# Window attention, forward and backward, on one core: weights loaded in rows and turned on TensorE, both projections ahead of attention in the first steps, weight-gradient groups of one quad at the end

## The chip, the cores and the metric

One core of a Trainium2 chip. The metric is the device time of one execution in microseconds, the median of several. Kernels are compared only within the same rounds.

## The reference, cut to what matters

```
qkv = window(x) @ wqkv                # x: 256 x 256 x 384, windows of 8 x 8 pixels
p   = softmax(q k^T * 384**-0.5)      # 64 x 64 per window
out = (p v) @ wo                      # first result
dx, dwqkv, dwo = vjp(grad_out)        # the other three
```

The kernel never forms q, k and v. It forms four products of weights once: A = scale Wq Wk^T, its transpose AT, B = Wv Wo, its transpose BT. It works on "quads" of eight windows (512 rows), 128 of them, in a software pipeline.

## The kernel before: the parts that count

A quad n needs its x and grad_out in rows (X, DO), both turned (XT, DOT, by DMA transpose), both projected (A on XT, BT on DOT, evicted to YHT) and the projections turned back (YH, by DMA transpose). All DMA transposes are issued on SyncE's queue, in program order. The kernel puts TensorE's products into eight PSUM banks (PS). Where new products go into a bank that is still full, the trace shows TensorE waiting until ScalarE (ACT) or VectorE (DVE) has evicted the old ones, that is, copied them out (three waits for ACT at the end of before, 2.3 us together). TM and PB are tiles of the softmax chain, OS and DXS hold the evicted first result and dX.

```python
def load_x(q, n):        # four DMAs of 96 KB, issued on the queue of engine q
    for t in range(4):
        q.dma_start(out=X[:, (n % NX) * 4 + t, :], in_=img(x, n, t))
# load_do: the same for DO.  turn_in(n, 0 or 1): SP.dma_start_transpose of X to XT, of DO to DOT
# turn_yh(n, a): SP.dma_start_transpose of YHT to YH

def step(n):
    T, S, A = n, n + 1, n + 2            # attention, scores, projections of three quads
    ...                                  # doT, doS, doA; doF: there is a finished group of three quads
    load_do(SP, n + 4); load_x(POOL, n + 4)
    turn_in(n + 3, 0); turn_in(n + 3, 1)
    if doS: scores(S)
    if doT: md(T)
    if doS: chain0(S)                    # softmax, first part (DVE)
    if doF:
        wgrad(g, k0)                     # weight gradient: 12 matmuls
    elif doA:
        proj(A, 0, (7, 4, 5, 3), ...)    # projection of X: 12 matmuls
        turn_yh(A, 0)
    if doS:
        chain2(S); chain3(S)             # softmax and its gradient (ACT, DVE, POOL)
    if doT:
        outs(T, 0, 0, ACT)               # result 0 into banks 0, 1; evicted by ACT to OS
        outs(T, 2, 2, ACT)               # banks 2, 3
        outs_st(T)
    if doF:
        wgrad(g, k0 + 1)
        if doA: ...                      # proj(A, 0), turn_yh(A, 0) here in full steps
    if doT:
        attn_all(T, S if doS else None)  # needs chain3 of T+1's scores to be off its bank (TM), and P of S (PB)
        dxs(T, 0)
        dxs_ev(T, 0, ACT)                # dX, first half, evicted by ACT to DXS
    if doA or A == 0:
        stack(A, 0, 0, 3)
        proj(A, 1, (3, 4, 5, 7), ...)    # projection of DO
        ...
        turn_yh(A, 1)
    if doT:
        dxs(T, 1)                        # second half; shares a bank with the first
        dxs_ev(T, 1, ACT)

# the start
for m in range(CK):
    SP.dma_start_transpose(out=wT[:, 0:2 * CK, ...], in_=wqkv[m * P:(m + 1) * P, 0:2 * C])   # Wq, Wk
load_x(ACT, 0)
ACT.dma_start(out=wo_sb[:], ...)
load_do(POOL, 0)
turn_in(0, 0)
for m in range(CK):
    SP.dma_start_transpose(out=wT[:, 2 * CK:, ...], in_=wqkv[m * P:(m + 1) * P, 2 * C:])     # Wv
turn_in(0, 1)
load_x(SP, 1)
...                                      # 14 matmuls that nobody reads (4.70 us)
wprod(A_sb, ...)
gate(A_sb[0:1, 2, 0:1])                  # POOL waits for A, then:
load_do(POOL, 1)
turn_in(1, 0); turn_in(1, 1)
proj(0, 0, ...); turn_yh(0, 0)
wprod(BT_sb, ...)
gate(BT_sb[0:1, 2, 0:1])
step(-2)                                 # load_do(SP, 2), load_x(POOL, 2), proj(0, 1), turn_yh(0, 1)
scores(0); chain0(0); chain2(0); chain3(0)
wprod(AT_sb, ...); wprod(B_sb, ...)
for n in range(-1, NQ): step(n)
...                                      # (cut) weights reloaded in rows at n == 4 for the end

# the end: weight-gradient groups of three quads, the last of two, all of it after the last step
for n in range(NQ, GQ * NG + GQ):
    for i in range(2):
        wgrad(n // GQ - 1, 2 * (n % GQ) + i, ...)
```

Of the kernel before, what the change touches and what calls it, by code (L numbers as in the profile page):

```python
# [11 lines left out]
BF16 = mybir.dt.bfloat16  # L12
# [4 lines left out]
def kernel(  # L17
# [11 lines left out]
    nc = tc.nc  # L29
    _, H, W, C = x.shape  # L30
    P = 128
    CK = C // P
# [3 lines left out]
    NQ = (H // 16) * NQC  # L36
    scale = float(C) ** -0.5
    GQ = 3
    NG = (NQ + GQ - 1) // GQ
    NX, ND, NXT, NDT, NYH, NTOK, NVW = 11, 5, 3, 2, 2, 3, 6  # L40
    PE, DVE, ACT, POOL, SP = nc.tensor, nc.vector, nc.scalar, nc.gpsimd, nc.sync

# [61 lines left out]
    def turn_yh(n, a):  # L104
        SP.dma_start_transpose(out=YH[:, n % NTOK, a, :, :],
                               in_=YHT[:, n % NYH, a, :, :].rearrange("p m t -> p (m t)"))

    def proj(n, a, banks, engs):
        wgt = A_sb if a == 0 else BT_sb
        src = (XT[:, n % NXT] if a == 0 else DOT[:, n % NDT]).rearrange("p (t m) k -> p m t k", m=CK)  # L110
        i = 0
        for mo in range(CK):
            for t0, t1 in ((0, 4),) if mo < CK - 1 else ((0, 2), (2, 4)):
                o = PS[:, banks[i], 0:P * (t1 - t0)]
                for m in range(CK):
                    mm(o.rearrange("p (t k) -> p t k", k=P), wgt[:, m, mo * P:(mo + 1) * P], src[:, m, t0:t1, :],
                       m == 0, m == CK - 1)
                ev(engs[i], YHT[:, n % NYH, a, mo, P * t0:P * t1], o)
                i += 1
# [134 lines left out]
            for w in range(2):  # L254
                POOL.dma_start(out=img(out_1, n, t)[8 * w:8 * w + 8], in_=DXS[64 * (1 - w):64 * (1 - w) + 64, n % 2, t, :])  # L255

    def wgrad(g, k, bank=7):
        quads = range(g * GQ, min(NQ, (g + 1) * GQ))
        which, ma = k // CK, k % CK
        tiles = [(q, t) for q in quads for t in range(4)]  # L260
        for i, (q, t) in enumerate(tiles):
            mm(PS[:, bank, 0:C], X[:, (q % NX) * 4 + t, ma * P:(ma + 1) * P], VW[:, (q % NVW) * 4 + t, which, :],
               i == 0, i == len(tiles) - 1)
        if g == 0:
            DVE.tensor_copy(out=ACC[:, k, :], in_=PS[:, bank, 0:C])
        else:
            DVE.tensor_tensor(out=GF[:, k, :] if g == NG - 1 else ACC[:, k, :], in0=PS[:, bank, 0:C],
                              in1=ACC[:, k, :], op=ALU.add)

    flat = VW[:].rearrange("p a b c -> p (a b c)")  # L270
    wT = flat[:, 0:JK * C].rearrange("p (j c) -> p j c", j=JK)
# [3 lines left out]
    bank = [0]  # L275
# [12 lines left out]
    def step(n):  # L288
        T, S, A = n, n + 1, n + 2
        doT, doS, doA = 0 <= T < NQ, 0 < S < NQ, 0 < A < NQ  # L290
        g, k0 = n // GQ - 1, 2 * (n % GQ)
        doF = 0 <= g < NG
        if 1 < n + 4 < NQ:
            load_do(SP, n + 4)
            load_x(POOL, n + 4)
        if 1 < n + 3 < NQ:
            turn_in(n + 3, 0)
            turn_in(n + 3, 1)
        if doS:
            scores(S)  # L300
        if doT:
            md(T)
        if doS:
            chain0(S)
        if doF:
            wgrad(g, k0)
        elif doA:
            proj(A, 0, (7, 4, 5, 3), (ACT, ACT, ACT, DVE))
            turn_yh(A, 0)
        if doS:  # L310
            chain2(S)
            chain3(S)
        if doT:
            outs(T, 0, 0, ACT)
            outs(T, 2, 2, ACT)
            outs_st(T)
        if doF:
            wgrad(g, k0 + 1)
            if doA:
                proj(A, 0, (3, 1, 2, 5), (ACT, ACT, ACT, DVE))  # L320
                turn_yh(A, 0)
        if doT:
            attn_all(T, S if doS else None)
            dxs(T, 0)
            dxs_ev(T, 0, ACT)
        if doA or A == 0:
            stack(A, 0, 0, 3)
            proj(A, 1, (3, 4, 5, 7), (ACT, ACT, ACT, DVE))
            stack(A, 1, 0, 2)
            stack(A, 1, 2, 3)  # L330
            turn_yh(A, 1)
        if doT:
            dxs(T, 1)
            dxs_ev(T, 1, ACT)
        elif S == 0:
            turn_p(S)
            turn_p_ev(S)

    def gate(ap):
        POOL.tensor_copy(out=ST[0:1, 3, 0:1], in_=ap)  # L340

    with tc.manual_schedule():

        wsrc = TM[:].rearrange("p t k -> p (t k)").bitcast(BF16)
        DVE.memset(wsrc, 0.0)
        ACT.activation(out=SS[:], in_=TM[:], func=ACTF.Exp)
        for m in range(CK):
            SP.dma_start_transpose(out=wT[:, 0:2 * CK, m * P:(m + 1) * P], in_=wqkv[m * P:(m + 1) * P, 0:2 * C])
        load_x(ACT, 0)
        ACT.dma_start(out=wo_sb[:], in_=wo.rearrange("(m p) n -> p m n", p=P))  # L350
        make_identity(nc, ident[:])
        load_do(POOL, 0)
        turn_in(0, 0)
        for m in range(CK):
            SP.dma_start_transpose(out=wT[:, 2 * CK:, m * P:(m + 1) * P], in_=wqkv[m * P:(m + 1) * P, 2 * C:])  # L355
        turn_in(0, 1)
        load_x(SP, 1)
        for i in range(14):
            mm(PS[:, 7, :], wsrc[:, 0:P], wsrc, True, True)
        wprod(A_sb, wT[:, 0:CK], wT[:, CK:2 * CK], True)  # L360
        gate(A_sb[0:1, 2, 0:1])
        load_do(POOL, 1)
        turn_in(1, 0)
        turn_in(1, 1)
        proj(0, 0, (0, 1, 2, 3), (ACT, DVE, ACT, DVE))
        turn_yh(0, 0)
        wprod(BT_sb, wo_sb, wT[:, 2 * CK:3 * CK], False)
        gate(BT_sb[0:1, 2, 0:1])
        step(-2)
        scores(0)  # L370
        chain0(0)
        chain2(0)
        chain3(0)
        wprod(AT_sb, wT[:, CK:2 * CK], wT[:, 0:CK], True)
        wprod(B_sb, wT[:, 2 * CK:3 * CK], wo_sb, False)
        for n in range(-1, NQ):
            step(n)
            if n == 4:
                for m in range(CK):
                    SP.dma_start(out=w_sb[:, m, :], in_=wqkv[m * P:(m + 1) * P, :])  # L380
                    SP.dma_start_transpose(out=woT_sb[:, :, m * P:(m + 1) * P], in_=wo[m * P:(m + 1) * P, :])


        b = 0
        for n in range(NQ, GQ * NG + GQ):
            for i in range(2):
                wgrad(n // GQ - 1, 2 * (n % GQ) + i, (3, 4, 5, 6, 7)[b % 5])
                b += 1

        def ep(o, lt, rr, dst, eng, sc):  # L390
            for mb in range(CK):
                mm(o, lt(mb), rr(mb), mb == 0, mb == CK - 1)
            if eng is ACT:
                ACT.activation(out=dst, in_=o, func=ACTF.Copy, scale=scale if sc else 1.0)  # L394
            elif sc:
                DVE.tensor_scalar(out=dst, in0=o, scalar1=scale, scalar2=None, op0=ALU.mult)
            else:
                DVE.tensor_copy(out=dst, in_=o)

        def tr(h):  # L400
            for mb in range(CK):
                pt = PS[:, h * CK + mb, :].bitcast(BF16)
                for ma in range(CK):
                    PE.transpose(pt[:, ma * P:(ma + 1) * P], GF[:, h * CK + ma, mb * P:(mb + 1) * P], ident[:])
                ev(DVE if mb % 2 == 0 else ACT, GFT[:, h * CK + mb, :], pt[:, 0:C])

        dw = flat[:, 0:CK * J].rearrange("p (m j) -> p m j", m=CK)
        dwo = flat[:, CK * J:CK * J + CK * C].rearrange("p (m j) -> p m j", m=CK)
        cut = lambda ma: slice(ma * P, (ma + 1) * P)
        tr(0)  # L410
        for ma in range(CK):
            ep(PS[:, 6 + ma % 2, 0:C], lambda mb: GF[:, mb, cut(ma)], lambda mb: w_sb[:, mb, C:2 * C],
               dw[:, ma, 0:C], DVE if ma == 1 else ACT, True)
        tr(1)
        for ma in range(CK):
            ep(PS[:, ma, 0:C], lambda mb: GFT[:, mb, cut(ma)], lambda mb: w_sb[:, mb, 0:C],
               dw[:, ma, C:2 * C], DVE if ma == 0 else ACT, True)
        SP.dma_start(out=out_2.rearrange("(m p) j -> p m j", p=P)[:, :, 0:2 * C], in_=dw[:, :, 0:2 * C])
        for ma in range(CK):
            ep(PS[:, 6 + ma % 2, 0:C], lambda mb: w_sb[:, mb, 2 * C + ma * P:2 * C + (ma + 1) * P],  # L420
               lambda mb: GF[:, CK + mb, :], dwo[:, ma, :], DVE if ma == 1 else ACT, False)
        ACT.dma_start(out=out_3.rearrange("(m p) n -> p m n", p=P), in_=dwo[:])
        for ma in range(CK):
            ep(PS[:, 3 + ma, 0:C], lambda mb: GFT[:, CK + mb, cut(ma)], lambda mb: woT_sb[:, mb, :],
               dw[:, ma, 2 * C:3 * C], DVE if ma == 1 else ACT, False)
            SP.dma_start(out=out_2[cut(ma), 2 * C:3 * C], in_=dw[:, ma, 2 * C:3 * C])
# [30 lines left out]
```

## Time and profile before

| | before |
|---|---|
| time, median of 3 | 1999.05 us (1997.54 to 2000.05) |
| TensorE busy | 1968.3 of 1997.9 us |
| a full step | 15.16 us, no wait of TensorE |
| first scores product of step 3 (the first full step) | 83.91 us |
| last scores product to the end of the span | 48.72 us |

The page's first part, busy time of each engine with its share of the span and its number of instructions:

```profile
PE 1968.3 (99%) x27496; PEld 1311.8 (66%) x27496; DVE 1341.4 (67%) x2962; ACT 1301.0 (65%) x2321; POOL 1291.7 (65%) x2312
```

One stretch of 15 us in the middle, in the windows view (columns: stretch, its length, busy time and instructions of PE, weight loads, DVE, ACT and POOL, granted TensorE clock (1.00 is full), DMA share, GB/s):

```profile
1000.00:1015.00 15.00, 15.00 (x215) 10.06 (x213) 10.28 (x23) 9.94 (x19) 10.07 (x18) 1.00 1.08 214
```

In the middle TensorE is busy for all of the 15 us at full clock. A change that leaves a full step alone can gain at the two ends only.

The start, in the timeline (start us, duration, engine, line, operation, and in brackets the idle time before it and what ended it). "SPq" is SyncE's queue issuing a DMA; a transpose XT<-X is one quad's turn.

```profile
11.07 1.42 SPq L101 DMA_TRANSPOSE XT<-X  x1
12.54 4.20 SPq L355 DMA_TRANSPOSE VW<-in_wqkv_dram  x3
16.90 1.46 SPq L101 DMA_TRANSPOSE DOT<-DO  x1
18.41 2.88 SPq L93 DMA_DIRECT2D X<-in_x_dram  x4
23.72 1.62 SPq L101 DMA_TRANSPOSE XT<-X  x1
...
31.80 4.34 POOL L93 DMA_DIRECT2D X<-in_x_dram  x8
...
38.64 2.39 SPq L101 DMA_TRANSPOSE XT<-X  x1
...
43.81 4.00 PE L75 MATMUL PS<-XT,A_sb 128*128 128x512 bf16 x12 [4.00 <-DMA XT<-X]
```

Quad 0's X is turned at 11.07, quad 1's at 23.72, quad 2's at 38.64. TensorE then waits 4.00 us for the last of these; it can project quad 2 only when the turn has landed, at 43.8.

Who held TensorE up from 36 to 90 us (waits: total us, times, longest), which is steps 0 to 2 and the start of step 3:

```profile
PE PS L75 <- DMA XT<-X: 4.7, 2, 4.0
PE PS L75 <- DVE TM L157: 2.4, 3, 1.4
PE PS L169 <- POOL PB L160: 1.2, 3, 0.6
...
```

The end: the waits from 1949 to 1990 us.

```profile
PE PS L75 <- ACT DXS L79: 2.3, 3, 0.9
PE PS L75 <- DVE ACC L267: 0.7, 2, 0.4
...
```

And the block of weight-gradient matmuls that stands behind the last step, in the timeline:

```profile
1974.61 11.86 PE L75 MATMUL PS<-VW,X 128*128 128x384 bf16 x72
```

TensorE waits 3.0 us in the last steps, and 11.9 us of work that could have filled those waits comes after them.

### The profile page before, as it was taken

The numbers are of one execution on the slowest core, as the hardware profiler recorded it, in microseconds if no ns is written. First come the engines' busy times: TensorE is split into PE (matmuls) and PEld (weight loads), VectorE is DVE, ScalarE is ACT, GpSimd is POOL, SyncE is SP. The second block draws the span as 40 slices with busy tenths as digits, with TensorE's granted clock in tenths as the row PEclk, the third lists the DMA queues.
The fourth block names the chain that finished last, engine by engine and source line by source line (L and its number), as shares of the span: only waits on it lengthen the run. The fifth ranks groups of instructions, "written<-read, shape, count | busy, mean of one in ns | idle before, by whom it ended". The sixth has DMA issues, their size and how long they took to land.

```text
span 1997.9 us, 68536 instructions
## 1 busy us (share of the span) xinstructions
PE 1968.3 (99%) x27496; PEld 1311.8 (66%) x27496; DVE 1341.4 (67%) x2962; ACT 1301.0 (65%) x2321; POOL 1291.7 (65%) x2312
## 2 busy tenths in 40 slices
PE   6999999999999999999999999999999999999998
PEld 3666666666666666666666666666666666666665
DVE  3676667667666666766666676676666667666664
ACT  2766666666666666666666666666666666666664
POOL 2766666666666666666666666666666666666653
PEclk8999999999999999999999999999999999999999
DMA  9999999999999999999999999999999999999993
GB/s 175 217 222 219 221 211 216 211 207 211 205 206 215 214 199 221 210 212 204 213 205 216 208 212 209 209 210 208 210 212 205 218 204 213 209 211 209 209 170 73
DMA packets 982127, 411.06 MB, mean 206 GB/s; under 512 B 865200, under 2 KB 956848, under 8 KB 981808
## 3 DMA queue, kind: packets, MB, share of 16 engines
q1 hardware_dynamic: 882128, 254.31, 78.4%
q0 software_dynamic: 98304, 151.39, 29.1%
q8 instruction: 215, 3.52, 0.7%
q10 hardware_dynamic: 1376, 0.98, 0.2%
q14 instruction: 104, 0.85, 0.2%
HBM read 101.84 MB, written 101.84 MB: 102 GB/s over the span
## 4 chain that ended last, share of the span: by engine, by line
PE 96%; DMA 1%; DVE 1%; ACT 1%; POOL 0%; SPq 0%; issue 0%; ACTq 0%; POOLq 0%; DVEq 0%
PE PS L75 95%; PE PS L169 2%; DMA X<-in_x_dram 1%; DMA XT<-X 0%; DMA DOT<-DO 0%; SPq L355 0%; DVE TM L157 0%; POOL PB L160 0%; ACT VW L394 0%; ACT YHT L79 0%; POOL UM L159 0%; ACT DXS L79 0%; POOL X L93 0%; ACT MD L79 0%; DVE PB L155 0%
## 5 line engine op out<-in xcount | busy, mean ns | idle before, releaser
L255 POOL DMA_DIRECT2D out_dram<-DXS x1024 | 577.9, 570 | 408.1 <-ACT DXS L79 380.5
L75 PE MATMUL PS<-VW,X 128*128 128x384 bf16 x3072 | 541.6, 326 | 0.0
L79 ACT CAST YHT<-PS 128x512 bf16<-128x512 f32 x767 | 370.5, 517 | 244.3 <-PE PS L75 229.8
L75 PEld LDWEIGHTS <-X 64*64 64x64 bf16 (+1 forms) x9216 | 380.4, 103 | 201.6 <-issue 1.0
L75 PEld LDWEIGHTS <-MD 128*128 128x128 bf16 x3840 | 338.5, 98 | 150.2 <-issue 2.8
L79 ACT CAST DXS<-PS 128x768 bf16<-128x768 f32 x256 | 204.3, 798 | 192.2 <-PE PS L75 190.8
L81 DVE CAST VW<-PS 128x384 bf16<-128x384 f32 (+1 forms) x384 | 253.4, 687 | 95.6 <-ACT VW L79 91.5
L81 DVE CAST YHT<-PS 128x256 bf16<-128x256 f32 (+1 forms) x257 | 109.3, 426 | 302.4 <-PE PS L75 295.1
L79 ACT CAST MD<-PS 128x512 bf16<-128x512 f32 x512 | 262.9, 600 | 52.0 <-PE PS L75 51.9
L75 PE MATMUL PS<-AT_sb,MD 128*128 128x384 bf16 (+2 forms) x2304 | 294.7, 273 | 1.8 <-ACT DXS L79 1.8
L93 POOL DMA_DIRECT2D X<-in_x_dram x504 | 270.5, 553 | 31.3 <-DMA out_dram<-DXS 17.8
L196 POOL DMA_DIRECT2D out_dram<-OS x512 | 275.0, 545 | 12.5 <-issue 9.2
L75 PE MATMUL PS<-XT,A_sb 128*128 128x512 bf16 (+1 forms) x1536 | 274.5, 329 | 6.9 <-DMA XT<-X 6.6
L75 PE MATMUL PS<-DOT,BT_sb 128*128 128x512 bf16 (+1 forms) x1536 | 270.8, 326 | 0.8 <-DVE YHT L81 0.5
L75 PE MATMUL PS<-B_sb,MD 128*128 128x384 bf16 x1536 | 271.1, 326 | 0.0
L81 DVE CAST MD<-PS 128x512 bf16<-128x512 f32 x256 | 165.1, 686 | 143.3 <-PE PS L75 143.3
L79 ACT CAST VW<-PS 128x384 bf16<-128x384 f32 (+1 forms) x384 | 212.6, 587 | 32.7 <-PE PS L75 5.8
L75 PEld LDWEIGHTS <-A_sb 128*128 128x128 bf16 x1536 | 151.3, 99 | 122.6 <-issue 10.3
L79 ACT CAST OS<-PS 128x768 bf16<-128x768 f32 x256 | 204.3, 798 | 25.9 <-PE PS L75 19.9
L75 PEld LDWEIGHTS <-BT_sb 128*128 128x128 bf16 x1536 | 150.4, 98 | 99.6 <-issue 1.3
L159 POOL TENSOR_TENSOR UM<-PB,ST 128x256 f32<-128x256 bf16 x128 | 78.2, 611 | 207.8 <-DVE ST L158 203.2
L75 PE MATMUL PS<-YH,PB 64*64 64x256 bf16 (+2 forms) x3072 | 194.6, 273 | 0.0
(54 smaller groups left out, 1971.4 us busy)
## 6 DMA issues: line engine op xcount, KB each, us to landing
out_dram<-OS POOLq DMA_DIRECT2D x512, 96.0 KB, 4.7
out_dram<-DXS POOLq DMA_DIRECT2D x1024, 48.0 KB, 3.8
X<-in_x_dram POOLq DMA_DIRECT2D x504, 96.0 KB, 4.0
DO<-in_grad_out_dram SPq DMA_DIRECT2D x504, 96.0 KB, 4.3
YH<-YHT SPq DMA_TRANSPOSE x256, 5.3
XT<-X SPq DMA_TRANSPOSE x128, 6.2
DOT<-DO SPq DMA_TRANSPOSE x128, 6.2
w_sb<-in_wqkv_dram SPq DMA_DIRECT2D x3, 288.0 KB, 5.4
```

The costliest lines, as they stand in the source:

```text
L75: PE.matmul(out, lhsT=lhsT, rhs=rhs, start=start, stop=stop, skip_group_check=True)
L79: ACT.copy(out=out, in_=in_)
L81: DVE.tensor_copy(out=out, in_=in_)
L93: q.dma_start(out=X[:, (n % NX) * 4 + t, :], in_=img(x, n, t))
L159: POOL.tensor_tensor(out=UM[:], in0=pb[:, 1], in1=bcast(3), op=ALU.mult)
L169: PE.transpose(bb[r, o:o + 64], PB[r, n % 2, a, t, :], ident[r, r])
L196: POOL.dma_start(out=img(out_0, n, t), in_=OS[:, n % 2, t, :])
L255: POOL.dma_start(out=img(out_1, n, t)[8 * w:8 * w + 8], in_=DXS[64 * (1 - w):64 * (1 - w) + 64, n % 2, t, :])
```

## The change

Three parts, each with its own aim:

- **Weights.** The six DMA transposes of weights go. The weights are loaded in rows by plain DMAs, and 27 transposes on TensorE turn them. First loads go out on three queues as before; that of Wo moves from ScalarE's queue to GpSimd's. The rows stay, so the reload at step 4 goes as well.
- **Order.** In the steps that have no weight-gradient work yet (-1 to 2), both projections stand ahead of attention, so that TensorE has work while the softmax chain of the next quad runs.
- **End.** The last two quads form groups of one, and what is left of the weight gradient fills slots in the last two steps.

```diff
-    NG = (NQ + GQ - 1) // GQ
+    groups = [tuple(range(q, q + GQ)) for q in range(0, NQ - GQ, GQ)]
+    groups += [(q,) for q in range(len(groups) * GQ, NQ)]
 ...
+    def fill(*banks):                    # pops finished pieces of weight gradient, up to 12 matmuls
+        left = 4 * GQ
+        for b in banks:
+            if todo and left >= 4 * len(groups[todo[0][0]]):
+                g, k = todo.pop(0)
+                wgrad(g, k, b)
+                left -= 4 * len(groups[g])
 ... in step(n):
+        early = not todo
-        if doF:
-            wgrad(g, k0)
-        elif doA:
+        if early and doA:
             proj(A, 0, (7, 4, 5, 3), (ACT, ACT, ACT, DVE))
             turn_yh(A, 0)
+        else:
+            fill(7)
 ... after outs(T):
-        if doF:
-            wgrad(g, k0 + 1)
-            if doA:
-                proj(A, 0, (3, 1, 2, 5), (ACT, ACT, ACT, DVE))
-                turn_yh(A, 0)
+        if not early:
+            fill(7)
+        if doA:
+            proj(A, int(early), (3, 1, 2, 5), (ACT, ACT, ACT, DVE))
+            turn_yh(A, int(early))
+        else:
+            fill(3, 1, 4)
         if doT:
             attn_all(T, S if doS else None)
 ... between the dX halves: proj(A, 1) only if not early, fill(3, 4, 5) where there is no quad A
 ... the start:
-            SP.dma_start_transpose(out=wT[:, 0:2 * CK, m * P:(m + 1) * P], in_=wqkv[m * P:(m + 1) * P, 0:2 * C])
+            SP.dma_start(out=w_sb[:, m, 0:2 * C], in_=wqkv[m * P:(m + 1) * P, 0:2 * C])
-        ACT.dma_start(out=wo_sb[:], in_=wo.rearrange("(m p) n -> p m n", p=P))
+        POOL.dma_start(out=wo_sb[:], in_=wo.rearrange("(m p) n -> p m n", p=P))
+        SP.dma_start(out=w_sb[:, :, 2 * C:], in_=wqkv.rearrange("(m p) j -> p m j", p=P)[:, :, 2 * C:])
         load_do(POOL, 0)
         turn_in(0, 0)
-        for m in range(CK):
-            SP.dma_start_transpose(out=wT[:, 2 * CK:, m * P:(m + 1) * P], in_=wqkv[m * P:(m + 1) * P, 2 * C:])
         turn_in(0, 1)
         load_x(SP, 1)
+        def wturn(j, eng): ...           # three PE.transpose into a bank, one eviction to wT
+        for j in range(2 * CK):
+            wturn(j, DVE if j % 2 == 0 else ACT)
         wprod(A_sb, wT[:, 0:CK], wT[:, CK:2 * CK], True)
 ... the end:
-        for n in range(NQ, GQ * NG + GQ):
-            for i in range(2):
-                wgrad(n // GQ - 1, 2 * (n % GQ) + i, (3, 4, 5, 6, 7)[b % 5])
+        for b in (3, 4, 5, 6, 7, 3):
+            fill(b)
```

More of the change, by code (lines that the diff above doesn't have):

```diff
@@ L255, in dxs_st, with wgrad @@
                 POOL.dma_start(out=img(out_1, n, t)[8 * w:8 * w + 8], in_=DXS[64 * (1 - w):64 * (1 - w) + 64, n % 2, t, :])
-    def wgrad(g, k, bank=7):
-        quads = range(g * GQ, min(NQ, (g + 1) * GQ))
+    def wgrad(g, k, bank):
         which, ma = k // CK, k % CK
-        tiles = [(q, t) for q in quads for t in range(4)]
+        tiles = [(q, t) for q in groups[g] for t in range(4)]
         for i, (q, t) in enumerate(tiles):
@@ L266, in wgrad @@
         else:
-            DVE.tensor_tensor(out=GF[:, k, :] if g == NG - 1 else ACC[:, k, :], in0=PS[:, bank, 0:C],
+            DVE.tensor_tensor(out=GF[:, k, :] if g == len(groups) - 1 else ACC[:, k, :], in0=PS[:, bank, 0:C],
                               in1=ACC[:, k, :], op=ALU.add)
+    todo = []
+    def fill(*banks):
[5 more added lines that the diff above has]
+                left -= 4 * len(groups[g])
     flat = VW[:].rearrange("p a b c -> p (a b c)")
@@ L290, in step @@
         doT, doS, doA = 0 <= T < NQ, 0 < S < NQ, 0 < A < NQ
-        g, k0 = n // GQ - 1, 2 * (n % GQ)
-        doF = 0 <= g < NG
+        early = not todo
         if 1 < n + 4 < NQ:
@@ L316, in step @@
             outs_st(T)
-        if doF:
-            wgrad(g, k0 + 1)
-            if doA:
-                proj(A, 0, (3, 1, 2, 5), (ACT, ACT, ACT, DVE))
-                turn_yh(A, 0)
+        if not early:
[5 more added lines that the diff above has]
+            fill(3, 1, 4)
         if doT:
             attn_all(T, S if doS else None)
+        if doA:
+            stack(A, 0, 0, 3)
+            if early:
+                stack(A, 1, 0, 3)
+        if doT:
             dxs(T, 0)
             dxs_ev(T, 0, ACT)
-        if doA or A == 0:
-            stack(A, 0, 0, 3)
+        if doA and not early:
             proj(A, 1, (3, 4, 5, 7), (ACT, ACT, ACT, DVE))
@@ L331, in step @@
             turn_yh(A, 1)
+        elif not doA:
+            fill(3, 4, 5)
         if doT:
@@ L337, in step @@
             turn_p_ev(S)
+        g = [g for g in groups if g[-1] == n]
+        if g:
+            todo.extend((groups.index(g[0]), k) for k in range(2 * CK))
     def gate(ap):
@@ L345, with wturn @@
         DVE.memset(wsrc, 0.0)
+        make_identity(nc, ident[:])
+        for m in range(CK):
+            SP.dma_start(out=w_sb[:, m, 0:2 * C], in_=wqkv[m * P:(m + 1) * P, 0:2 * C])
         ACT.activation(out=SS[:], in_=TM[:], func=ACTF.Exp)
-        for m in range(CK):
-            SP.dma_start_transpose(out=wT[:, 0:2 * CK, m * P:(m + 1) * P], in_=wqkv[m * P:(m + 1) * P, 0:2 * C])
         load_x(ACT, 0)
-        ACT.dma_start(out=wo_sb[:], in_=wo.rearrange("(m p) n -> p m n", p=P))
-        make_identity(nc, ident[:])
+        POOL.dma_start(out=wo_sb[:], in_=wo.rearrange("(m p) n -> p m n", p=P))
+        SP.dma_start(out=w_sb[:, :, 2 * C:], in_=wqkv.rearrange("(m p) j -> p m j", p=P)[:, :, 2 * C:])
         load_do(POOL, 0)
         turn_in(0, 0)
-        for m in range(CK):
-            SP.dma_start_transpose(out=wT[:, 2 * CK:, m * P:(m + 1) * P], in_=wqkv[m * P:(m + 1) * P, 2 * C:])
         turn_in(0, 1)
         load_x(SP, 1)
-        for i in range(14):
+        for i in range(12):
             mm(PS[:, 7, :], wsrc[:, 0:P], wsrc, True, True)
+        def wturn(j, eng):
+            pt = PS[:, bank[0] % 6, :].bitcast(BF16)
+            bank[0] += 1
+            for m in range(CK):
+                PE.transpose(pt[:, m * P:(m + 1) * P], w_sb[:, m, j * P:(j + 1) * P], ident[:])
+            ev(eng, wT[:, j, :], pt[:, 0:C])
+        for j in range(2 * CK):
+            wturn(j, DVE if j % 2 == 0 else ACT)
         wprod(A_sb, wT[:, 0:CK], wT[:, CK:2 * CK], True)
@@ L364 @@
         turn_in(1, 1)
+        for j in range(2 * CK, 3 * CK):
+            wturn(j, DVE)
         proj(0, 0, (0, 1, 2, 3), (ACT, DVE, ACT, DVE))
@@ L368 @@
         gate(BT_sb[0:1, 2, 0:1])
-        step(-2)
+        stack(0, 0, 0, 3)
+        load_do(SP, 2)
+        load_x(POOL, 2)
+        proj(0, 1, (3, 4, 5, 7), (ACT, DVE, ACT, DVE))
+        stack(0, 1, 0, 2)
+        stack(0, 1, 2, 3)
+        turn_yh(0, 1)
         scores(0)
@@ L379 @@
                 for m in range(CK):
-                    SP.dma_start(out=w_sb[:, m, :], in_=wqkv[m * P:(m + 1) * P, :])
                     SP.dma_start_transpose(out=woT_sb[:, :, m * P:(m + 1) * P], in_=wo[m * P:(m + 1) * P, :])
-        b = 0
-        for n in range(NQ, GQ * NG + GQ):
-            for i in range(2):
-                wgrad(n // GQ - 1, 2 * (n % GQ) + i, (3, 4, 5, 6, 7)[b % 5])
-                b += 1
+        for b in (3, 4, 5, 6, 7, 3):
+            fill(b)
         def ep(o, lt, rr, dst, eng, sc):
```

## The prediction

> **What bounds the kernel.** Between 90 and 1955 us TensorE never waits: the windows show it busy throughout, and the chain of waits repeats one step of 15.16 us. The change leaves the order of work inside a full step as it was, so these 123 or so steps should cost the same. Only the ends can move.
>
> **The start.** Until about 80 us DMA binds. In the timeline SyncE's queue issues without a gap from 23.7 us (turn of quad 1's X) to beyond step 3, slowed by the DMA engines (DMA share 1.0 to 1.3). TensorE waits for what it delivers: 1.8, 4.0 and 0.7 us for turned X (at 30.2, 43.8, 72.7). So what counts is when that stream starts. It starts late: weight transposes slow X of quad 0 (last landing 11.0 us, 7.8 after issue); three more take the queue from 12.5 to 16.7; then come the turn of DO, the load of X of quad 1 (18.4 to 21.3), its landing, and its turn at 23.7.
>
> The change replaces six weight transposes by four plain loads (about 0.6 us of issue each). [...] I count bytes: weights, X and DO of quad 0 are 1.97 MB, at an estimated 270 GB/s (this trace's larger packets run at 245 to 290) done at 9 to 10 us. Estimated sequence: Wq and Wk landed 6.5; X of quad 0 landed 8 to 9; turn of X 8.7, of DO 10, load of X of quad 1 11.5 to 14.4, its turn at 17: 6.8 us earlier.
>
> Added on TensorE: 27 transposes of about 0.075 us (nine took 0.67 us at the end of before) and nine evictions of 0.35 to 0.48 us, where TensorE idles anyway (7.5 us for weights). Product A ends near 11 us, not 16.9; projection 0 starts 3 us earlier.
>
> **Both projections ahead of attention, steps 0 to 2.** They fill waits for the softmax chain (0.2, 1.4, 0.7 us) and for P (up to 0.5). But in step 2 the projection of DO now needs DOT of quad 4, which landed at 77.4 us, about 0.8 us after TensorE would ask. As DMA sets the pace, I count 0.2 us.
>
> **The end.** From 1955 to 1975 us TensorE idles 3.0 us (0.9 twice for the dX eviction, 0.5, 0.4). After it stand 72 weight-gradient matmuls in 11.9 us; 48 of them move into the last two steps and fill gaps. Work is the same, only gaps count: 1.8 us, the rest being new waits on banks 3, 1 and 4. Dropping the reload of weights at step 4 brings nothing.
>
> **Sum.** 6.8 + 0.2 + 1.8 = 8.8: 1990.2 us, range 1984.5 to 1995. Chances: faster by over 2% 0.01, within 2% 0.985, slower 0.005.
>
> **What would show it.** Turn of quad 1's X near 17 us; SyncE's queue gapless from there; the first full step 7 us earlier; steps of 15.16 us; a wait of about 1 us for DOT in step 2; 3.9 us of matmuls after the last dX product, not 11.9; TensorE idle in the last 45 us down by 2.
>
> **What would make it wrong.** Plain loads delaying X of quad 0 beyond 9 us; TensorE at half clock before product A ([...] before, the clock fell to 0.5 at 11 us), delaying DO of quad 1, which waits for A; the freed DMA stream catching up faster (more gain); a longer DOT wait.

Two passages on how the hardware behaves, which no run here shows, are cut and marked. That the first loads, on whatever queue, can be counted as bytes at one rate is the author's estimate, on which the 9 to 10 us and so the 6.8 us rest (in before's DMA records, packets of 768 to 16384 bytes moved at 243 to 286 GB/s: their bytes over their mean time, times 16 engines). Two readings of before's trace: that the DMA engines slowed SyncE's queue (it took 1.42 us to issue a turn of X at 11.07 us, 2.39 us at 38.64), and that the weight transposes slowed quad 0's X (it landed up to 7.8 us after issue; in the changed kernel, without them, up to 7.6).

## The result

The median went from 1998.93 us (4 runs, 1997.54 to 2000.05) to 1994.92 us (4 runs, 1993.43 to 1997.09). A ratio in this document is the mean time of one kernel's fast runs over the mean of the other's of the same rounds, so it is not quite the ratio of the medians quoted. Here it is 0.9981, with an interval of 0.9964 to 0.9998: about 4 us faster, where 8.8 were forecast. A second measurement of the same kernel (below) gave 0.9983.

The start after the change, timeline:

```profile
10.37 1.59 SPq L102 DMA_TRANSPOSE XT<-X  x1
12.14 2.45 SPq L102 DMA_TRANSPOSE DOT<-DO  x1
14.63 2.97 SPq L94 DMA_DIRECT2D X<-in_x_dram  x4
19.66 1.47 SPq L102 DMA_TRANSPOSE XT<-X  x1
...
30.47 4.60 POOL L94 DMA_DIRECT2D X<-in_x_dram  x8
...
34.64 1.92 SPq L102 DMA_TRANSPOSE XT<-X  x1
...
42.03 3.69 PE L76 MATMUL PS<-XT,A_sb 128*128 128x512 bf16 x12 [5.54 <-DMA XT<-X]
```

Quad 0's X is turned at 10.37 us, 0.7 us earlier than before, not 2.4. Quad 1's is turned at 19.66, 4.1 us earlier, not 6.8. Quad 2's is issued at 34.64, 4.0 us earlier, but TensorE starts on it at 42.03, only 1.8 us earlier: from issue to use it took 7.4 us here and 5.2 before. TensorE's wait for it has grown from 4.00 to 5.54 us. The first full step starts at 82.01 us, 1.9 earlier than before.

In stretches of 3 us (TensorE's busy time is the first figure after the length; the last three columns are clock, DMA share and GB/s):

```profile
9.00:12.00 3.00, 1.47 (x15) 1.02 (x14) 0.89 (x3) 1.47 (x3) 1.44 (x4) 1.00 0.16 40
...
18.00:21.00 3.00, 2.88 (x18) 1.47 (x17) 2.78 (x6) 0.37 (x1) 0.18 (x1) 1.00 0.25 65
...
39.00:42.00 3.00, 0.00 (x0) 0.00 (x0) 0.06 (x1) 0.00 (x0) 0.00 (x0) 0.50 1.33 154
42.00:45.00 3.00, 2.97 (x9) 1.17 (x9) 0.00 (x0) 0.80 (x2) 0.00 (x0) 0.50 1.15 249
```

The DMA engines stand nearly still twice (shares of 0.16 and 0.25), each time around the moment at which SyncE's queue has waited for a load of X to land and issues its turn. And while TensorE waits for quad 2, its clock falls to half, and it is still at half when the work arrives.

The waits from 36 to 90 us:

```profile
PE PS L76 <- DMA XT<-X: 5.5, 1, 5.5
PE PS L76 <- ACT DXS L80: 2.7, 3, 0.9
PE PS L76 <- ACT OS L80: 2.7, 3, 0.9
```

The waits for the softmax chain (TM, PB) are gone, 3.6 us together. In their place stand six waits of 0.9 us for ScalarE: the projection of DO now follows the outputs into banks that ScalarE has yet to clear (OS), and the second dX half now follows the first with nothing between them (DXS).

The end, waits from 1946 to 1985 us:

```profile
PE PS L76 <- ACT DXS L80: 0.5, 1, 0.5
PE PS L76 <- DVE ACC L267: 0.3, 1, 0.3
...
```

And the block behind the last step:

```profile
1977.55 4.06 PE L76 MATMUL PS<-VW,X 128*128 128x384 bf16 x24
```

From the last scores product to the end of the span it is 45.99 us, against 48.72 (spans are printed to 0.1 us, so such figures are good to 0.05): 2.7 us, more than the 1.8 forecast. So of the 5.0 us between these two spans 2.7 come from the end, 1.9 from before step 3, and 0.4 from the middle, half of it one step of 15.37 us in before.

### The profile page after: what moved, and what is told of

Read it like the earlier page. It is cut to its first block, busy times and chain, and to the rows that moved or that the text cites. A ratio compares the mean times of both kernels' runs of the same rounds, so it can differ in the third digit from the quotient of the medians.

```text
span 1992.9 us, 68590 instructions
## 1 busy us (share of the span) xinstructions
PE 1965.5 (99%) x27521; PEld 1312.0 (66%) x27521; DVE 1346.8 (68%) x2971; ACT 1301.9 (65%) x2323; POOL 1295.0 (65%) x2313
## 4 chain that ended last, share of the span: by engine, by line
PE 97%; DMA 2%; ACT 1%; DVE 0%; POOL 0%; issue 0%; ACTq 0%; DVEq 0%; SPq 0%
PE PS L76 95%; PE PS L170 2%; DMA X<-in_x_dram 1%; DMA XT<-X 1%; DMA out_dram<-DXS 0%; ACT DXS L80 0%; ACT VW L428 0%; POOL X L94 0%; ACT OS L80 0%; DVE BT_sb L297 0%; ACT YHT L80 0%; POOL out_dram L256 0%; ACTq L94 0%; ACT MD L80 0%; DVE ST L144 0%
## 5 line engine op out<-in xcount | busy, mean ns | idle before, releaser
L80 ACT CAST YHT<-PS 128x256 bf16<-128x256 f32 (+1 forms) x766 | 369.9, 518 | 251.4 <-PE PS L76 234.5
```

What stands on the lines that cost most here:

```text
L80: ACT.copy(out=out, in_=in_)
```

## The experiments

The theory (A): steps 0 to 2 run from the moment when quad 2's turned X lands, and from there TensorE's own chain of work and evictions takes the same time in both kernels, because the new order swaps one kind of wait for another. The start of SyncE's stream counts only as far as it moves that landing. Rivals: (B) DMA sets the pace of all of steps 0 to 2; (C) the new order is a gain that something else hides. Two more suspects are added on the way: the loads that run beside the turn (in the changed kernel 559 KB of GpSimd's queue landed between its issue and its use), and the half clock.

The table collects from each trace: when the turn of X of quads 1 and 2 was issued, when TensorE began to project quad 2, when step 3 began (its scores product), the difference of these two, the half-clock periods between 36 and 90 us, and the time from the last scores product to the end of the span. "after again" is the changed kernel once more. The means are of each run's fast executions, and of before in the same rounds. Each trace is one execution.

| run | turn q1 | turn q2 | project q2 | step 3 | difference | half clock | end | mean, before's mean | ratio |
|---|---|---|---|---|---|---|---|---|---|
| before | 23.72 | 38.64 | 43.81 | 83.91 | 40.10 | 41.8 to 48.7 | 48.72 | | |
| after | 19.66 | 34.64 | 42.03 | 82.01 | 39.98 | 38.5 to 45.3 | 45.99 | 1995.1, 1998.9 | 0.9981 |
| after again | 20.08 | 35.56 | 44.05 | 85.39 | 41.34 | 39.2 to 49.5 | 45.97 | 1995.9, 1999.2 | 0.9983 |
| end_only | 23.10 | 38.15 | 44.01 | 83.90 | 39.89 | 41.0 to 47.8 | 46.14 | 1997.1, 2000.6 | 0.9983 |
| order_only | 23.52 | 39.02 | 45.04 | 86.25 | 41.21 | 42.8 to 49.6 | 48.71 | 1999.7, 1998.6 | 1.0004 |
| old_order | 20.21 | 34.88 | 43.11 | 83.18 | 40.07 | 42.0 to 48.9 | 46.05 | 1996.0, 2000.6 | 0.9977 |
| banks | 20.50 | 35.73 | 42.35 | 81.93 | 39.58 | 39.2 to 46.0, 80.1 to 83.5 | 45.95 | 1994.5, 2000.6 | 0.9970 |
| turn_first | 19.93 | 31.63 | 39.65 | 80.81 | 41.16 | 38.4 to 45.2 | 45.99 | 1994.2, 2000.6 | 0.9969 |
| defer_x4 | 19.71 | 34.29 | 40.28 | 83.08 | 42.80 | 39.8 to 43.2, 67.1 to 70.6 | 45.98 | 1994.5, 1999.2 | 0.9976 |
| warm | 19.67 | 34.08 | 43.85 | 84.59 | 40.74 | 44.0 to 47.4 | 45.98 | 1995.3, 1999.2 | 0.9980 |
| warm30 | 20.59 | 34.72 | 44.66 | 83.06 | 38.40 | none | 46.02 | 1996.0, 1999.8 | 0.9979 |
| x1_before | 19.23 | 33.10 | 41.24 | 80.20 | 38.96 | none | 48.72 | 1996.0, 1999.8 | 0.9980 |
| x1_first | 15.41 | 30.10 | 38.36 | 77.69 | 39.33 | none | 45.99 | 1991.7, 1999.2 | 0.9964 |
| x1_old_order | 15.95 | 31.70 | 39.51 | 78.28 | 38.77 | none | 46.01 | 1992.2, 1998.6 | 0.9969 |
| x1_split | 15.43 | 30.80 | 36.23 | 78.18 | 41.95 | 53.9 to 57.3 | 46.04 | 1991.2, 1998.6 | 0.9964 |
| best | 16.44 | 31.28 | 38.44 | 80.61 | 42.17 | 53.4 to 60.3 | 45.96 | 1991.1, 1998.6 | 0.9964 |

The spread of the end column within its two groups is mostly the rounding of the spans. All outputs were correct in all runs.

### The order, undone in the changed kernel

```diff
-        if doA:
-            proj(A, int(early), (3, 1, 2, 5), ...)   # early: projection of DO
+        if doA and not early:
+            proj(A, 0, (3, 1, 2, 5), ...)
 ...
-        if doA and not early:
+        if doA:
             proj(A, 1, (3, 4, 5, 7), ...)            # between the dX halves, in all steps
```

> The changed kernel with one part undone: in the first steps the projection of DO stands again between the two dX halves. Theory A (from the landing of quad 2's turned X, about 42 us, TensorE's own chain of work and evictions sets the time; the new order only swaps 0.9 us waits for ScalarE's evictions for waits for the softmax chain): time within 0.7 us of the changed kernel (1994.9), steps 1 and 2 at 13.1 to 13.6 us against 13.35, waits for TM and PB back, the 0.89 us waits for OS and DXS gone, no wait for turned X or DO in steps 1 and 2. Rival B (DMA sets the pace of steps 0 to 2): about the same time, but with waits for turned X or DO of about 1 us in steps 1 and 2. Rival C (the new order is a gain that is hidden elsewhere): 2 us or more slower than the changed kernel.

Ratio 0.9977 (0.9964 to 0.9991), against 0.9981 and 0.9983 with the new order. From quad 2's projection to step 3 it is 40.07 us, against 39.98. Steps 1 and 2 took 13.53 and 13.46 us (from scores to scores), against 13.35 and 13.34. The softmax waits are back and no DMA wait stands in steps 1 and 2. Theory A holds, B falls for these two steps (TensorE waits for no DMA there), C falls by the trace (the intervals of the times alone would still allow 2 us). Step 3 started only 0.7 us earlier than before in this trace, with the whole weight part in place.

### The order alone, on the kernel before

```diff
+        elif doA:                                    # no weight gradient yet
+            proj(A, 1, (3, 1, 2, 5), (ACT, ACT, ACT, DVE))
+            turn_yh(A, 1)
         if doT:
             attn_all(T, S if doS else None)
```

> The kernel before with only the order of the first steps changed (both projections ahead of attention). Theory A: within 0.7 us of before; 40 us from the landing of quad 2's turned X to step 3; the waits for TM and PB give way to waits of 0.89 us for OS and DXS, and a wait for quad 4's turned X or DO in step 2. Rival C: 2 us or more faster than before.

Ratio 1.0004 (0.9992 to 1.0016): nothing. Its waits from 36 to 90 us:

```profile
PE PS L75 <- DMA XT<-X: 5.8, 1, 5.8
PE PS L75 <- ACT OS L79: 2.7, 3, 0.9
PE PS L75 <- ACT DXS L79: 2.7, 3, 0.9
PE PS L75 <- DVE TT L81: 1.5, 1, 1.5
PE PS L169 <- POOL PB L160: 0.4, 1, 0.4
```

The swap is the same as in the changed kernel: 5.4 us of waits for ScalarE for 3.6 us (in before) of softmax waits. The expected DMA wait in step 2 did not come.

### The end alone, on the kernel before

The edit is the first two hunks of the change (groups, fill) and its loop at the end, with the old order and the old start.

> The kernel before, with only the end changed (weight-gradient groups of one quad, spread over the last two steps). Expected from the two traces: from the last scores product to the end of the span 46.0 us against 48.7, so 2.7 us faster than before (1996.3), and nothing else changed: first full step at the same time as before. Rival (end worth only the 1.8 us predicted or less, the rest of the difference between the traces being chance): 1997.2 or more.

Ratio 0.9983 (0.9971 to 0.9996), 3.5 us by the means, and the trace places 2.6 us (48.72 to 46.14) behind the last scores product; step 3 starts at 83.90, as before (83.91). The end is between 45.95 and 46.14 us in all 13 traces that have the change, and 48.71 or 48.72 in the three that have not. This part is settled, at 2.6 to 2.7 us.

### Other banks for the early projection of DO

```diff
-            proj(A, int(early), (3, 1, 2, 5), ...)
+            proj(A, int(early), (7, 4, 5, 1) if early else (3, 1, 2, 5), ...)
```

> The changed kernel, with the banks of the early projection of DO changed from 3,1,2,5 to 7,4,5,1, so that it does not wait for ScalarE to evict the output banks 2 and 3. Theory A: three waits of 0.89 us go, some of it may come back as a softmax wait; 1.5 to 2.7 us faster than the changed kernel (1992.2 to 1993.4), steps 1 and 2 near 12.5 us. Rival B: no gain (within 0.5 us), waits for DMA appear in place of the waits for OS.

Ratio 0.9970, 1.1 to 1.3 thousandths (2.2 to 2.6 us) below the changed kernel, which the intervals do not separate. In the trace the waits for OS are gone and step 1 took 12.60 us, as expected. Step 2 took 14.40 us: a wait of 0.8 us for PB appeared and the clock fell to half at 80.1 us, so step 3 started at 81.93, as in the changed kernel. The waits are real and removable, but what is gained can be lost one step later. For the total it is inconclusive.

### Quad 2's turns ahead of the load of quad 3's DO

```diff
-            load_do(SP, n + 4); load_x(POOL, n + 4)
-            turn_in(n + 3, 0); turn_in(n + 3, 1)
+            turn_in(n + 3, 0); turn_in(n + 3, 1)     # in step -1 only: turns first
+            load_do(SP, n + 4); load_x(POOL, n + 4)
```

> The changed kernel, in step -1 SyncE's queue issues the two turns of quad 2 ahead of the load of DO of quad 3, which took 31.55 to 34.5 us before it. Theory A: quad 2's turned X is issued near 31.6 and lands near 38 to 39 us, not 42; what follows is TensorE's own chain, so the first full step starts about 3 us earlier: 1992 us. Rival B: the late loads turn into DMA waits in steps 1 or 2, within 1 us of the changed kernel.

Ratio 0.9969. The turn was issued at 31.63 and TensorE started on it at 39.65, 2.4 us earlier than in the changed kernel's first trace. Of this 1.2 us reached step 3 (80.81 against 82.01). The difference column has it: 41.16, not 39.98. The half clock ended at 45.2 us, as late as in the first trace, so more of the work after the earlier landing ran at half clock. That is what made the clock a suspect. Theory A had expected 3 us, B less than 1; the mean came out 1.9 to 2.9 us under the changed kernel's, relative to before, which the intervals do not separate from either.

### The changed kernel again, as a control

> The changed kernel once more, as the control of this call: 4 us faster than before (ratio 0.998), quad 2's turned X landing at 42 us give or take 1, 40.0 us from there to step 3, 46.0 us from the last scores to the end.

Ratio 0.9983 (0.9971 to 0.9996), with executions from 1992.63 to 1998.01 us. In this trace quad 2's X was issued at 35.56 and reached TensorE at 44.05, later than in before's trace; the clock was half from 39.2 to 49.5, and step 3 started at 85.39, later than before's 83.91. The end made up for it. So the weight part's gain at the start is not even certain in a single execution, and the 1.9 us between the first two traces are no measure of it. The expectations missed: 41.34 and not 40.0 us from there to step 3, and 44.05 and not 42 for the landing.

### Matmuls that nobody reads, ahead of the wait: 16, then 30

```diff
+        if T == 0:
+            for i in range(16):                      # warm30: 30
+                mm(PS[:, 7, :], w_sb[:, 0, 0:P], w_sb[:, 0, 0:512], True, True)
         if early and doA:
             proj(A, 0, (7, 4, 5, 3), ...)
```

> The changed kernel with 16 matmuls of 512 columns whose result nobody reads, in step 0 ahead of the projection that waits for quad 2's turned X. In every trace so far TensorE idles over 4 us there and the granted clock is 0.5 for 6.8 us from about 38.5. Theory A with the clock: the matmuls (3.4 us at full clock) fit into the wait, the clock stays at 1, the projection takes 2.1 us and not 3.7, so from the landing to step 3 it is 38.4 us, not 40.0: 1.6 us faster than the changed kernel. Rival (the clock does not matter, DMA paces the steps): no change within 0.5 us, DMA waits appear.

By the table, the half clock had begun at 38.4 to 42.0 us in the six traces up to then, and TensorE's wait ahead of it was 4.00 us in before, 4.1 in old_order, 4.9 in end_only and 5.54 in after. Ratio 0.9980: no gain, a miss. The trace in windows, from 42 us:

```profile
42.00:44.00 2.00, 0.15 (x1) 0.10 (x1) 0.00 (x0) 0.00 (x0) 0.00 (x0) 0.99 0.80 83
44.00:47.40 3.40, 3.40 (x12) 1.58 (x11) 0.00 (x0) 1.37 (x3) 0.00 (x0) 0.50 1.23 262
```

And the projection in the timeline:

```profile
43.85 3.79 PE L76 MATMUL PS<-XT,A_sb 128*128 128x512 bf16 x12 [2.57 <-DMA XT<-X]
```

The unread matmuls ended 2.57 us before the landing, and the clock fell right when the work arrived. So this run did not test the suspect. (Full clock came back after 3.5 us of work here, and in the changed kernel's two traces after 3.3 and 5.4 us.) The second run covers the wait:

> The changed kernel with 30 unread matmuls (6.5 us at full clock) in place of the 16 of the run warm, so that TensorE is busy up to the landing of quad 2's turned X, when that is at 42 to 44 us. If the half clock is a cost of its own: no half clock between 38 and 50 us, projection, outputs and what follows at full clock, 38.4 us from the projection to step 3 where it was 40.0 to 41.3, and 1 to 2.5 us faster than the changed kernel (ratio to before 0.9983), minus up to 1 us where the matmuls overrun the landing. If the clock is of no weight: no change within 0.5 us.

Its timeline:

```profile
38.40 6.42 PE L76 MATMUL PS<-w_sb 128*128 128x512 bf16 x29 [0.16 <-issue]
44.66 2.11 PE L76 MATMUL PS<-XT,A_sb 128*128 128x512 bf16 x12
```

Now there is no half clock between 36 and 90 us, the projection takes 2.11 us and not 3.7 to 4.0, and from it to step 3 it is 38.40 us, the figure expected, against 39.98 and 41.34. By that the half clock costs 1.6 to 2.7 us of an execution of the changed kernel: from the projection to step 1 it is 13.29 and 14.36 us in its two traces and 11.71 here (the other 0.3 us of after_again lie in step 2, at full clock). That is half of the 3.3 and 5.4 us of work that ran at half clock. The time gained little (0.9979 against 0.9983), because in exchange the projection begins only when the unread matmuls end, at 44.66. What this shows is a cost, not a cure.

### The load of quad 4's X put off

```diff
             load_do(SP, n + 4)
-            load_x(POOL, n + 4)
+            if n != 0:
+                load_x(POOL, n + 4)                  # quad 4's: after chain3 of step 0
```

> The changed kernel with the load of quad 4's X (step 0) put behind quad 1's softmax on GpSimd's queue, where nothing needs it for 10 us. The loads of X of quads 3 and 4 (issued 30.5 to 35 us) share the DMA engines with the turn of quad 2's X (issued 34.6, landed 41.9, 7.3 us; 5.2 before). If they are what slowed it: it lands 1.3 to 2 us earlier and step 3 starts that much earlier, about 1.7 us faster than the changed kernel. If not: landing and time as in the changed kernel within 0.5 us.

In the changed kernel, from 34.64 to 42.03 us, the DMA share was 1.18 at 208 GB/s. That the loads and the turn share the engines is a reading of that; it was not tested by itself. Ratio 0.9976. Quad 2's turn was issued at 34.29 and TensorE started on it at 40.28: 6.0 us from issue to use, against 7.4 and 8.5 in the two traces of the changed kernel. This fits the suspicion that loads of X of quads 3 and 4 slow the turn. The time gained was 1.4 us by the means of the same rounds, within the intervals. But steps 1 and 2 took 15.71 and 13.93 us, with a wait of 1.28 us for PB and a second half-clock period, so step 3 came no earlier. It is one trace; the share of those loads in the late landing stays likely, not shown.

### The load of quad 1's X ahead of the turns of quad 0

```diff
         load_do(POOL, 0)
+        load_x(SP, 1)
         turn_in(0, 0)
         turn_in(0, 1)
-        load_x(SP, 1)
```

> The changed kernel with the load of quad 1's X issued on SyncE's queue ahead of the two turns of quad 0, into the time in which the queue waits for X of quad 0 (2.6 to 10.4 us). The turn of quad 1's X then follows directly, at 14.6 us and not 19.7. The step of my prediction that is in question (an earlier start of SyncE's stream moves the first full step by as much): 5 us faster than the changed kernel. Theory A: what counts is the landing of quad 2's turned X, which shares the engines with loads that GpSimd issues only after quad 0's softmax (30.5 us, set by TensorE and VectorE), so the gain is well under 5 us: 1 to 3 us.

Ratio 0.9964 (0.9950 to 0.9977). In the same rounds the mean is 4.2 us below that of the changed kernel (1991.68 against 1995.87). The timeline:

```profile
2.61 6.69 SPq L94 DMA_DIRECT2D X<-in_x_dram  x4
...
15.41 1.72 SPq L102 DMA_TRANSPOSE XT<-X  x1
...
30.10 1.50 SPq L102 DMA_TRANSPOSE XT<-X  x1
...
38.36 2.12 PE L76 MATMUL PS<-XT,A_sb 128*128 128x512 bf16 x12
```

The load fills the time in which SyncE's queue waited for quad 0's X. Quad 1's turn is issued at 15.41. TensorE no longer waits for quad 2 at all (no bracket at 38.36), there is no half clock, and step 3 starts at 77.69. Theory A had put the gain at 1 to 3 us and the plain "earlier stream, earlier steps" at 5; 4.2 lies between them, and the intervals allow either. What A missed, by this trace, is that ending the wait also ends the half clock.

### The same move on the kernel before

```diff
         load_do(POOL, 0)
+        load_x(SP, 1)
         turn_in(0, 0)
 ...
         turn_in(0, 1)
-        load_x(SP, 1)
```

> The kernel before, with only the load of quad 1's X moved ahead of the turns of quad 0 on SyncE's queue; its weights are still transposed by DMA. If the early start of quad 1's turn is what counts and the weights are of little weight: the turn of quad 1's X is issued near 19 us, not 23.7, quad 2's turned X lands early enough to shorten or end TensorE's wait of 4 us there, 2 to 4 us faster than before. If the weight transposes themselves hold the start (six of them on the same DMA engines and the same queue, and product A not before 16.9 us, which lets in DO of quad 1): within 1 us of before, and the gain of x1_first over the changed kernel needs both parts together.

Ratio 0.9980 (0.9961 to 0.9999), 3.8 us by the means, of which 0.8 us comes from a single execution of before at 2006.38 us. One moved line, with all six weight transposes still in DMA, gives about as much as the whole change under study. The timeline:

```profile
19.23 1.79 SPq L101 DMA_TRANSPOSE XT<-X  x1
...
41.24 2.11 PE L75 MATMUL PS<-XT,A_sb 128*128 128x512 bf16 x12 [1.52 <-DMA XT<-X]
```

Quad 1's turn is issued at 19.23 us, as early as in the changed kernel. TensorE waits 1.5 us for quad 2's X (and 1.5 us for quad 4's), and the clock does not fall after 36 us. So the weight transposes by themselves did not hold the start; the place of that load did. One thing in this trace is not explained: product A began at 9.53 us there and at 13.35 in before, although its weights are loaded in the same way. (The last two loads of quad 0's X went out at 5.51 us and not at 2.50, so fewer loads ran beside the weight transposes; that this is the reason was not tested.) Projection 0 gained only 0.6 us by it (15.58 against 16.18) and the scores of quad 0 nothing (24.52 against 24.62). But the load of quad 1's DO, which waits for A, went out 3.8 us earlier, at 13.28. At before's 17.10 it would have landed near 22.6 us and held the turn behind quad 1's X by some 1.4 us (an estimate, from the median of 3.9 us from issue to landing in before's page). That much of the gain may be owed to it.

### On top of it: old order, a split projection, turns first

x1_old_order has the order of before in x1_first:

> The kernel x1_first with the projection of DO back between the dX halves in the first steps. Here DMA does not hide what the order is worth in steps 0 and 1. Theory A (the new order swaps waits of 0.9 us for OS and DXS for waits for the softmax chain): within 0.7 us of x1_first, steps 0 and 1 at 13.2 to 13.6 us with waits for TM and PB. Rival C (the new order is a gain): 2 us or more slower than x1_first, steps of 14 us.

Ratio 0.9969 (0.9957 to 0.9981) against 0.9964. From quad 2's projection to step 3 it is 38.77 us against 39.33; steps 0 to 2 took 13.39, 13.52 and 13.45 us. The order is worth nothing here either, where no DMA wait hides it: the softmax waits (4.3 for TM and 1.5 for PB) stand where ScalarE's stood.

x1_split cuts the early projection of DO, two thirds ahead of attention in banks 7 and 4, one third between the dX halves:

```diff
+        if doA and early:
+            proj(A, 1, (7, 4), (ACT, ACT), (0, 1))   # ahead of attention
 ...
+        if doA and early:
+            proj(A, 1, (4, 5), (ACT, DVE), (2,))     # between the dX halves
+            turn_yh(A, 1)
```

> The kernel x1_first (load of quad 1's X ahead of the turns), with the early projection of DO cut in two: two thirds of it ahead of attention, in banks 7 and 4 that wait for no eviction, one third between the two dX halves. It aims at the six waits of 0.89 us for ScalarE (OS, DXS) in steps 0 to 2, 5.3 us together. Theory A with the DMA limit close behind (in x1_first TensorE already waited 0.9 us for quad 4's turned X at 66.0 us): steps 0 and 1 get shorter but the wait for quad 4's X grows to 2 to 4 us, only step 2's own waits are gained: 0.5 to 2 us faster than x1_first (1990 to 1991 where before is 1998.5). If TensorE's chain alone counts: 4 us faster than x1_first.

Ratio 0.9964, the same as x1_first, where 0.5 to 2 us less were expected. Its waits from 36 to 90 us:

```profile
PE PS L76 <- DMA XT<-X: 5.5, 2, 4.5
PE PS L170 <- POOL PB L161: 0.3, 1, 0.3
PE PS L76 <- ACT DXS L80: 0.2, 1, 0.2
```

The waits for ScalarE and for the softmax chain are nearly all gone, and step 0 took 12.45 us. It turned into a wait of 4.5 us for quad 3's turned X in step 1, with a half-clock period behind it, and one of 1.0 us for quad 4's. Here rival B is right: with its own waits removed, TensorE meets the DMA limit. I had expected the large wait at quad 4; it came one quad earlier.

The run best adds the early turns of quad 2 to it:

> The kernel x1_split with, in addition, the two turns of quad 2 ahead of the load of DO of quad 3 in step -1. As quad 2's turned X was not waited for any more in x1_first, theory A expects nothing from it: within 0.7 us of x1_split. If it is 1.5 us or more faster, the order of SyncE's queue still sets the time.

Ratio 0.9964: nothing more, as expected. x1_first is the simplest kernel of those that beat both, 7.5 us below before by the means of its rounds.

## Why the prediction was wrong, point by point

- **What bounds the kernel, and steps of 15.16 us: right.** Between step 3 and the last steps only 0.4 us moved, half of it one step of 15.37 us in before.
- **The weights, 6.8 us: the step that failed.** The prediction said of the start of SyncE's stream: "So what counts is when that stream starts", and let all of the 6.8 us pass to the first full step. Old order against end_only in the same rounds, both with the new end, gives 1.1 us for the weight part (means 1996.03 and 1997.13). With the load of quad 1's X moved, x1_old_order less end_only and x1_before, each by its difference from before in its own rounds, gives 6.4 - 3.5 - 3.8 = -0.9 us (-0.1 without the one execution of before at 2006.38). The 1.1 is uncertain by some 3 us, the other figure by more. So the weight part is worth about zero to one, and not 6.8. Three things took the place of the assumption:
  - The stream started 4.1 us earlier, not 6.8. Quad 0's X was turned at 10.37 us, not 8.7 (a risk that the prediction had named: beyond 9 us), and the turn of DO and the load of quad 1's X behind it ran in series, with the DMA engines nearly idle twice. The weights had been in front of that series, but the series itself was the longer part. x1_before shows it: moving the one load gave the same start (19.23 us) with the weight transposes in place.
  - The start of the stream did not carry to the landing of quad 2's turned X: 42.03 and 44.05 us in two traces, against 43.81. The turn was issued 3 to 4 us earlier and took 7.4 and 8.5 us, not 5.2. This is so across the table: from issue to use it took 5.2 to 6.0 us in the three traces that issued it after 38 us, and 6.6 to 9.8 in the seven that issued it between 31.6 and 35.7 and waited for it, but for defer_x4 (6.0). The loads of X of quads 3 and 4 start after quad 0's softmax on GpSimd's queue, at 30.47 us (31.80 before), so an earlier turn runs beside them, and defer_x4 is the run that took one of them away. The DMA records of the kept traces show how much of it landed during the turn, from issue to use: GpSimd's queue brought 307 to 389 KB in the three late turns, 295 in defer_x4, 559 and 698 in the changed kernel's two traces, and 495 to 787 in the seven. But the DMA engines as a whole also moved less per microsecond, 208 GB/s in both traces of the changed kernel against 244 in before. At 244 GB/s the 205 and 344 KB more of the changed kernel are worth 0.8 and 1.4 us (an estimate) of the 2.2 and 3.3 us by which its turn was longer. So these loads are likely a part of the cause; what lowered the rate stays open.
  - TensorE, done earlier with its own preparation, waited longer there (5.5 and 6.9 us, 4.0 before), and the half clock took 1.6 to 2.7 us of what followed (warm30). Before had that cost too, with 4.9 us of work at half clock after its wait, so it explains why the steps were slow in both and not why the gain was missing. The prediction named the half clock as a risk, but ahead of product A, where it did not come in the changed kernel's two traces (in turn_first it did, from 7.7 to 11.1 us).
- **The order, 0.2 us: right in size by luck, wrong in mechanism.** It was put down to DMA setting the pace and a wait for DOT in step 2. No such wait came. The gain of the softmax waits (3.6 us in before; 5.8 in x1_old_order, where no DMA wait or half clock hides part of them) is paid for by six waits of 0.89 us for ScalarE, which the prediction did not look for, although the diff shows both: bank 3, which the outputs have just filled, and the bank that the dX halves share. order_only (1.0004), old_order and x1_old_order show it three times.
- **The end, 1.8 us: the mechanism right, the size off.** It measured 2.6 to 2.7 us. TensorE's waits there fell from 3.0 to 0.8 us; I had allowed over 1 us for new waits on banks 3, 1 and 4, and only 0.3 us came. Some 0.4 us of the gain is not waiting: TensorE's busy time behind the last scores product fell from 41.44 to 41.07 us, for which the record shows no cause.
- **The block behind the last dX product:** 4.06 us, 3.9 forecast. Right.
- **The extra work on TensorE:** 27 transposes, 2.0 us in all, and product A was ready at 10.5 us. Right. But projection 0 started only 1.2 us earlier (14.99 us against 16.18), not 3, and it took 3.56 us: TensorE had waited 4.5 us for quad 0's turned X, and the clock was at half from 14.6 to 18.0. The early product A was of little use, as the turned X that it multiplies landed only then.

## What to carry to other kernels

In the ramp of a pipeline, follow one item from load to first use and ask which waits in that series can overlap; moving one load that needed nothing (3.8 us in x1_before) gave about as much as the whole change (4 us), the rewriting of how the weights come in included. An earlier start of a queue is worth only what reaches the next thing that the busy engine waits for (here 4.0 us at the issue of quad 2's turn became 1.8 us at its use), so measure that landing, not the issue. When work is moved to fill one wait, look at what it stood between in its old place, and at which banks it enters in the new one.

## What the traces show of the clock, of transposes and of turns

- The fall to half clock. In the changed kernel and in before it fell to 0.50 when TensorE had waited for 2.0 us, in waits for quad 2's X of 5.54 and 4.00 us. In warm the wait was 2.57 us, after 3.4 us of dense matmuls at full clock, and the granted clock was 0.50 from 44.0 to 47.4 us. It also fell after shorter waits close together: in banks (at 80.1 us) and defer_x4 (at 67.1 us) no wait in the 3.4 us before the fall was longer than 0.89 and 1.28 us, and TensorE was busy for 1.73 and 1.53 us of them. In x1_before no half clock followed a wait of 1.52 us. What decides it these runs do not show.
- The return to full clock. After the wait for quad 2's turned X it came 3.0 us (defer_x4) to 5.8 us (old_order) after work had come back. Half-clock periods of 3.4 us (warm), 6.8 (the changed kernel) and 10.2 us (its second trace) occur.
- Transposes on TensorE. In the changed kernel's trace one of 128x128 in bf16 is recorded with 219 ns, and 27 of them took 2.0 us, 75 ns each, as they overlap; the clock was 1.00 through them. In turn_first it was 0.50 from 7.7 to 11.1 us, and 16 of them took 1.89 us, not 1.07.
- A DMA transpose beside other loads. From issue to use the same 384 KB turn took 5.2 us in before and 7.4 and 8.5 us in two traces of the changed kernel.
